# A new order for the opening of a retention-and-two-MLPs kernel: loads, first products, masks, and where the retention units are visited

## The chip, the core and the metric

The kernel runs on one core of one Trainium2 chip. The metric is the device time of one launch in microseconds (us), taken as the median of the runs shown.

## What is computed

Retention (a decaying running sum of outer products of keys and values, read by queries) over 768 steps, for 4 batches and 8 heads of 64; its output, 3072 tokens of 512 features, goes through two two-layer networks. Weights arrive as 64-bit floats.

```
state = zeros(B, H, D, D)
for t in range(S):                                  # S = 768, D = 64
    state = gamma * state + k[t] (outer) v[t]       # gamma = 1 - 2**(-5-h), per head h
    y[t] = q[t] @ state / sqrt(D)
x = y as (3072, 512)
h = x @ w_in1;  x = (h * cos(h)) @ w_out1           # 512 -> 2048 -> 512
h = x @ w_in2;  out = where(h > 0, h, exp(min(h, 0)) - 1) @ w_out2
```

## The kernel before

**Tiling.** Tokens are cut into 6 blocks of 512 and 24 units of 128 (4 units to a block). The hidden width of 2048 is cut into 8 tiles `j` of 256. Products of fp32 quality are made from three TensorE products of a high and a low part (`PARTS`), so the first layer's product for one block, one `j` and one half (128 hidden features) takes 12 matmuls of 128x512, four chunks of three. They stand on line 778 (`product1`). From about 329 us on, TensorE does the second layers and the second network (lines 862 and 1039) by a seven-product scheme.

**Units.** A unit of retention is worked off in steps that each use 64x64 tiles of TensorE: `scores` (keys against queries, line 639, and for later units the sums of keys and values, line 594), `carried` (queries against the running state, line 693) and `values` (line 728). The function `meet` is a *visit*: it does `carried` of unit n, `scores` of unit n+1 and `values` of unit n, then loads unit n+3. VectorE multiplies the scores by a mask (line 658), GpSimd writes one small fence per unit between `carried` and `values` (line 705), and ScalarE and VectorE split the result into high and low parts (lines 365 and 370). The first four units are special: for them a unit is one chunk of 128 features over all four batches, so chunk `kc` of block 0 needs unit `kc` alone. The sums of these four (`first_sums`, line 594) are taken in two pairs, each pair in a PSUM buffer of its own that VectorE then copies to the state (line 615).

**Weights.** `to_f32` loads a half of a weight tile as raw 64-bit words (512 KB), ScalarE makes two passes over it, a third pass runs on GpSimd (line 410) for three halves of the opening and on ScalarE otherwise, and VectorE joins them (line 417). `first_weights` then splits the tile into high and low parts.

**What sets the order.** A planner (`Plan.run`) takes the steps in the order in which the code records them, gives each a due time, and writes the instructions of every engine. TensorE's order is the recorded one. In the opening the load queue goes by ranks (`opening`). Zero products (`warm`, line 1116) fill TensorE's idle time at the start. Buffers come from pools: in PSUM, `eg` has three buffers (scores, sums, hidden products) and `f` has two (zeros, `carried`/`values`, second layer). The function `dma` sends nearly all loads and stores through SP's queue (line 360), and a load waits for the one eight places ahead of it.

**Where visits stand.** A list of (block, half step, function, unit) at the end of the code puts a visit in front of a half product or between its two halves. Units 6 and 23 are split: their `carried` is a visit of its own.

## Time and profile before

| what | value |
|---|---|
| median of 3 runs | 1020.47 us (1020.46 to 1022.87) |
| profiled execution | 1020.92 us, span 1019.1 us |
| TensorE busy | 1011.3 us, 99% of the span |
| VectorE busy | 780.0 us, 77% |
| ScalarE busy | 636.2 us, 62% |
| GpSimd busy | 163.1 us, 16% |
| granted TensorE clock | 1.00 |

The span runs from the first to the last instruction of the profiled execution; 1.8 us of its time lie around the span. A busy share is an average over stages, and the stage that the change touches is the first 330 us, and of that mostly the first 30. In the rows, a line of the timeline gives the start, the length of the group, the engine, the line, the operation with its output and inputs, and in brackets how long the engine sat idle before it and who ended that. One 64x64 product of the program stands as two records, so a step of 16 products shows as x32.

### The profile page before, as it was taken

What the parts mean: (1) busy time and instruction counts of PE and PEld (TensorE: products, weight loads), DVE (VectorE), ACT (ScalarE), POOL (GpSimd) and SP (SyncE); (2) the same over time, 40 slices, a digit from 0 to 9 for tenths busy, and PEclk for the clock granted to TensorE, in tenths of its full rate; (3) what the DMA queues carried; (4) which work ended last, traced back from release to release, by engine and by line L of the source; (5) the groups of instructions that cost most, each with busy time, mean ns of one, the idle gap of its engine ahead of it and who ended that gap; (6) DMA issues with size and microseconds to landing.
All of it is one profiled execution on the core that took longest, in us unless ns stands there. A gap on an engine that the chain in (4) does not pass through costs nothing.

```text
span 1019.1 us, 17949 instructions
## 1 busy us (share of the span) xinstructions
PE 1011.3 (99%) x7088; PEld 831.1 (82%) x7090; DVE 780.0 (77%) x928; ACT 636.2 (62%) x801; POOL 163.1 (16%) x163
## 2 busy tenths in 40 slices
PE   8999999999999999999999999999999999999998
PEld 5888888888888888888888888888888888888887
DVE  7998887798699768566669998978899866565453
ACT  5985458655896544444455788988998644444442
POOL 2222321222032101000001242332221100000000
PEclk9999999999999999999999999999999999999999
DMA  9997999999999999999977579899968999999862
GB/s 349 354 341 291 353 334 379 345 351 357 335 363 342 340 344 333 367 320 357 350 231 254 208 255 340 303 335 350 337 248 303 315 365 335 361 316 349 286 201 88
DMA packets 110244, 323.17 MB, mean 317 GB/s; under 512 B 8657, under 2 KB 9041, under 8 KB 107601
## 3 DMA queue, kind: packets, MB, share of 16 engines
q1 hardware_dynamic: 110016, 321.95, 88.5%
q8 instruction: 55, 0.90, 0.4%
q14 instruction: 29, 0.23, 0.1%
q10 hardware_dynamic: 144, 0.10, 0.0%
HBM read 195.66 MB, written 126.35 MB: 316 GB/s over the span
## 4 chain that ended last, share of the span: by engine, by line
PE 98%; DMA 2%; DVE 0%; POOL 0%; SPq 0%; issue 0%; POOLq 0%
PE eg L1039 45%; PE eg L778 26%; PE eg L862 16%; PE f L862 6%; DMA c<-in_weights 2%; PE f L693 1%; PE eg L594 1%; PE f L728 1%; PE eg L639 1%; POOL c L410 0%; PE eg L728 0%; SPq L360 0%; DVE c L417 0%; DVE hl L370 0%; DVE h L370 0%
## 5 line engine op out<-in xcount | busy, mean ns | idle before, releaser
L1039 PE MATMUL eg<-hl,w 128*128 128x512 f32 (+1 forms) x2022 | 457.4, 388 | 0.0
L1039 PEld LDWEIGHTS eg<-hl,w 128*128 128x128 f32 x2022 | 378.8, 188 | 78.4
L365 ACT ACTIVATE hl<-ld 128x1024 fp32r<-128x1024 f32 x168 | 177.8, 1060 | 221.0 <-PE eg L1039 218.5
L370 DVE TENSOR_TENSOR hl<-ld,hl 128x1024 fp32r<-128x1024 f32 x168 | 209.8, 1252 | 129.0 <-ACT hl L365 128.4
L778 PE MATMUL eg<-hl,w 128*128 128x512 f32 x1152 | 269.5, 392 | 0.7 <-DVE hl L370 0.7
L778 PEld LDWEIGHTS eg<-hl,w 128*128 128x128 f32 x1152 | 214.0, 188 | 46.8 <-DVE hl L370 1.0
L365 ACT ACTIVATE c<-c 128x512 f32<-128x512 f32 (+3 forms) x197 | 160.1, 850 | 29.5 <-DVE c L370 13.5
L370 POOL TENSOR_TENSOR c<-c 128x512 f32<-128x512 f32 (+2 forms) x91 | 101.2, 1118 | 434.4 <-DMA c<-d 164.3
L365 ACT ACTIVATE c<-eg 128x1024 int32<-128x1024 f32 (+2 forms) x95 | 86.5, 910 | 57.4 <-PE eg L778 49.8
L370 DVE TENSOR_TENSOR c<-c 128x512 f32<-128x512 f32 (+2 forms) x161 | 109.7, 692 | 16.2 <-DMA c<-d 9.9
L862 PE MATMUL eg<-hl,w 128*128 128x512 f32 x432 | 109.5, 390 | 0.0
L862 PEld LDWEIGHTS eg<-hl,w 128*128 128x128 f32 x432 | 80.9, 188 | 17.5 <-DVE c L370 0.4
L862 PE MATMUL eg<-ld,w 128*128 128x512 f32 x288 | 73.2, 390 | 0.0
L809 DVE SCALAR_TENSOR_TENSOR c<-eg,c 128x1024 f32<-128x1024 f32 x48 | 58.6, 1221 | 18.0 <-ACT c L365 17.7
L365 ACT ACTIVATE c<-c,quarter_turn 128x1024 f32<-128x1024 f32 x48 | 55.2, 1150 | 25.6 <-DVE c L809 24.9
L370 DVE TENSOR_TENSOR c<-c,eg 128x1024 f32<-128x1024 f32 x48 | 58.3, 1215 | 12.5 <-ACT c L365 12.2
L862 PEld LDWEIGHTS eg<-ld,w 128*128 128x128 f32 x288 | 53.9, 188 | 11.8 <-ACT h L365 0.6
L365 ACT ACTIVATE w<-c 128x1024 fp32r<-128x1024 f32 (+3 forms) x63 | 54.2, 886 | 12.9 <-DVE c L370 5.3
L485 DVE SCALAR_TENSOR_TENSOR w<-c,w 128x1024 fp32r<-128x1024 f32 (+3 forms) x51 | 54.2, 1077 | 2.0 <-ACT w L365 2.0
L365 ACT ACTIVATE ends<-c 128x512 int16<-128x512 uint32 x64 | 50.0, 787 | 2.3 <-DMA c<-in_weights 2.3
L862 PE MATMUL f<-hl,w 128*128 128x512 f32 x144 | 36.6, 389 | 0.0
L862 PE MATMUL f<-ld,w 128*128 128x512 f32 x144 | 36.5, 389 | 0.0
(76 smaller groups left out, 675.4 us busy)
## 6 DMA issues: line engine op xcount, KB each, us to landing
d<-c SPq DMA_DIRECT2D x205, 512.0 KB, 5.2
ld<-d SPq DMA_DIRECT2D x84, 1024.0 KB, 8.3
c<-d SPq DMA_DIRECT2D x93, 512.0 KB, 6.3
c<-in_weights SPq DMA_DIRECT2D x64, 512.0 KB, 6.8
ld<-in_attn SPq DMA_DIRECT2D x19, 1024.0 KB, 7.0
d<-h SPq DMA_DIRECT2D x48, 256.0 KB, 6.4
out<-c SPq DMA_DIRECT2D x11, 512.0 KB, 7.9
ld<-in_attn SPq DMA_DIRECT2D x3, 512.0 KB, 7.6
```

What stands on the lines that cost most here:

```text
L365: plan.op("ACT", us, lambda: bank_of(nc.scalar.activation(out=out_(), in_=in_(), func=func, **kw), r), r, w, lag)
L370: return bank_of(e.tensor_tensor(out=out_(), in0=a(), in1=b(), op=op), r)
L485: plan.op("DVE", 0.065 + 0.267 * (hi - lo), lambda: nc.vector.scalar_tensor_tensor(out=w.t[:, lo:hi, 1, :], in0=view(), scalar=turn, in1=h ...
L594: nc.tensor.matmul(out=sc.t[j * D:(j + 1) * D, e, lo:lo + D], lhsT=u.t[r, 1536 + h0:1536 + h0 + D], rhs=u.t[r, 1024 + h0:1024 + h0 + D], s ...
L639: ins = nc.tensor.matmul(out=sc.t[e * HC:(e + 1) * HC, j, at:at + cols], lhsT=u.t[r, 512 + h0 + cs * HC:512 + h0 + cs * HC + HC], rhs=u.t[ ...
L693: ins = nc.tensor.matmul(out=xps[e].t[o * D:(o + 1) * D, a2, ch * HC:(ch + 1) * HC], lhsT=s[r, e * 2 + a2, :], rhs=q[r, 2 * a2 + e, ch * H ...
L728: ins = nc.tensor.matmul(out=x_out(e)[o * D:(o + 1) * D, a2, lo:lo + cols], lhsT=u.t[r, h0:h0 + D], rhs=pt_of()[r, j, at:at + cols], start ...
L778: nc.tensor.matmul(out=h.t[:, half * TB:(half + 1) * TB], lhsT=quarter(j, quads[kc // 2], wpart, kc % 2), rhs=(xh, xl)[xpart].t[:, kc, :], ...
L809: plan.op("DVE", 1.134, lambda: nc.vector.scalar_tensor_tensor(out=g.t, in0=h.t, scalar=1.0 / TWO_PI, in1=n(), op0=ALU.mult, op1=ALU.subtract,
L862: bank_of(nc.tensor.matmul(out=out_(), lhsT=w.t[:, i, wpart, kc * P:(kc + 1) * P], rhs=x.t[:, xpart, kc, :], start=(start and n == 0), sto ...
L1039: bank_of(nc.tensor.matmul(out=to.t[:, at:at + c1 - c0], lhsT=w[:, A_OF[p], wpart, i * P:(i + 1) * P], rhs=hl.t[:, gpart, k, c0:c1], start ...
```

## The change

- **First loads** go by a table, `FIRST_LOADS`, in place of the order unit by unit.
- **First queries unscaled.** The first four units' queries are no longer multiplied by the decay table; the decay of the query's row goes into the masks, whose tables are built from a new small table (`rise`) with VectorE and two ScalarE copies. The decay table itself is loaded and built later.
- **First products** go by `FIRST_PRODUCTS`: the scores first, 16 zeros behind the first, and the products of `j` 0 and 1, chunk by chunk, all ahead of the first sums (before: `j` 0 alone).
- **First slices by quarters.** The quarters of the first tiles are packed in another order, and the tile of `j` 1 is split in two steps as that of `j` 0 was; GpSimd does the third pass for five halves, not three.
- **First values** use the two small `f` buffers in place of one `eg` buffer, and are split in two halves on ScalarE and VectorE.
- **Odd blocks in reverse**: blocks 1 and 3 go through `j` from 7 to 0, and the results of `j` 5 to 7 of the block before stay in SBUF (`HELD`), so that six loads of 512 KB fall away.
- **Visits** stand in a table with 24 entries in place of 25: unit 6 is no longer split.
- The planner counts the cost of a change between small and full TensorE tiles. This changes no instruction by itself.

```diff
+FIRST_LOADS = (
+    ("tab",), ("qk", 1), ("qk", 0), ("v", 0), ("w", 0, 0), ("qk", 2), ("w", 1, 0), ("k", 1),
...
+FIRST_PRODUCTS = (
+    ("s", 0), ("z", 16), ("s", 1), ("x", 0), ("s", 2), ("x", 1),
+    ("h", 0, 1, (0,)), ("z", 4), ("x", 2), ("h", 0, 0, (0,)), ("s", 3), ("h", 0, 0, (1,)),
...
+HELD = 3
+VISITS = (
+    (4, "sums_of", 0), (4, "sums_of", 2), (5, "scores_of", 4), (6, "meet", 4), (8, "meet", 5),
...
-            if (layer, io) == (0, 0) and (j, hh) in ((0, 0), (0, 1), (1, 0)):
+            if (layer, io) == (0, 0) and (j, hh) in BY_POOL:
...
-        ends = [4 * j + 2] * (j == 0) + [4 * j + 4]
+        ends = [4 * j + 2] * (j < 2) + [4 * j + 4]
...
-        xps = xps_of.pop(n) if c else [Buf("eg", [P, 2, TB])]
+        xps = xps_of.pop(n) if c else [Buf("f", [P, 2, P]) for _ in range(2)]
...
-        for e in range(2) if c else (slice(0, 2),):
+        for e in range(2):
...
-        quads = ((0, 1), (3, 2))[fi]
+        quads = ((0, 2), (1, 3))[fi]
...
+            if sb < NSB - 1 and j >= NJ - HELD:
+                held[j] = g
...
-        y = Buf("c", [P, 2 * TB])
+        y = held.pop(j, None)
         t4 = Buf("h", [P, TB])
-        dma(4, lambda: y.t, lambda: gd[layer, sb].t[:, j, 2:4, :],
-            [gd[layer, sb][j * NP + 2, j * NP + 4]], [y], lag)
+        if y is None:
+            y = Buf("c", [P, 2 * TB])
+            dma(4, lambda: y.t, lambda: gd[layer, sb].t[:, j, 2:4, :],
+                [gd[layer, sb][j * NP + 2, j * NP + 4]], [y], lag)
...
+        for at, by in ((0, by_own), (1, by_late)):
+            tt("DVE", 0.37, lambda at=at, slots_at=slots_at: slots_at(at), up, by, ALU.mult,
+               [rise, tab_at, cst[604, 740]], [own])
+        tt("DVE", 0.37, lambda slots_at=slots_at: slots_at(0), lambda slots_at=slots_at: slots_at(0),
+           lambda: tri(2, 2), ALU.mult, [own, tab_at], [own])
+        act(0.33, lambda slots_at=slots_at: slots_at(2), lambda slots_at=slots_at: slots_at(0), [own], [own])
...
-    warm(12)
-    scale_unit(0, which=(0,))
+    warm(ZEROS)
...
+    first_h = [Buf("eg", [P, 2 * TB]) for _ in range(2)]
+    for name, n, *at in FIRST_PRODUCTS:
...
-    split = (6, 23)
...
+            j = NJ - 1 - at if blk in (1, 3) else at
```

What that does to the engines is shown at three places.

SP's queue, the first loads, before. `ld_123`, `ld_144`, `ld_156` and `hl_193` are units 0 to 3, and `c_...` are weight halves; a row of 1024 is queries and keys, one of 512 is values or, the second time, the keys by token.

```order
L360 DMA ld_123<-in_attn 128x1024
L360 DMA ld_123<-in_attn 128x512
L360 DMA c_142<-in_weights 128x1024
L360 DMA ld_144<-in_attn 128x1024
L360 DMA ld_144<-in_attn 128x512
L360 DMA c_150<-in_weights 128x1024
L360 DMA ld_156<-in_attn 128x1024
L360 DMA ld_156<-in_attn 128x512
L360 DMA hl_193<-in_attn 128x1024
L360 DMA hl_193<-in_attn 128x512
```

The same place after; units 0 to 3 are `ld_123`, `ld_141`, `ld_148` and `hl_227`, and the seventh row is unit 1's keys by token.

```order
L393 DMA ld_123<-in_attn 128x1024
L393 DMA ld_141<-in_attn 128x1024
L393 DMA ld_123<-in_attn 128x512
L393 DMA c_144<-in_weights 128x1024
L393 DMA ld_148<-in_attn 128x1024
L393 DMA c_172<-in_weights 128x1024
L393 DMA ld_141<-in_attn 128x512
L393 DMA ld_148<-in_attn 128x512
L393 DMA ld_141<-in_attn 128x512
L393 DMA w_121<-in_tab 128x96
L393 DMA c_207<-in_weights 128x1024
L393 DMA hl_227<-in_attn 128x1024
```

Unit 1's values were the fifth load and are now the ninth; unit 0's queries and keys are the first in both, though the table names unit 1 first.

TensorE, the first sums, before, with what each waits for (DVE is VectorE, Pool GpSimd, DMAHW a load).

```order
L594 MATMUL eg<-ld 64x64 [waits DMAHW5_49,PE_49,Pool_49]
L594 MATMUL eg<-ld 64x64 x15
L594 MATMUL eg<-ld 64x64 [waits DMAHW6_49]
L594 MATMUL eg<-ld 64x64 x15
L594 MATMUL eg<-ld 64x64 [waits DMAHW7_49,PE_49]
L594 MATMUL eg<-ld 64x64 x15
L594 MATMUL eg<-hl 64x64 [waits DMAHW0_49]
L594 MATMUL eg<-hl 64x64 x15
```

The same place after.

```order
L626 MATMUL eg<-ld 64x64 [waits DMAHW0_49,PE_49]
L626 MATMUL eg<-ld 64x64 x15
L626 MATMUL eg<-ld 64x64 [waits DMAHW7_49,Pool_49]
L626 MATMUL eg<-ld 64x64 x15
L626 MATMUL eg<-ld 64x64 [waits DVE_49,DMAHW7_49,PE_49,Pool_49]
L626 MATMUL eg<-ld 64x64 x15
L626 MATMUL eg<-hl 64x64 [waits DMAHW1_49]
L626 MATMUL eg<-hl 64x64 x15
L808 MATMUL eg<-hl,w 128x512 [waits DVE_49]
```

The third unit's sums wait for VectorE now: two of the three `eg` buffers hold hidden products, and the second pair takes the buffer of the first, which VectorE has to copy out.

TensorE, two visits in the middle of the first network, before: the small steps of a visit and the products between.

```order
L693 MATMUL f<-ld,w 64x64 x16
L594 MATMUL eg<-ld 64x64 x16
L639 MATMUL eg<-ld 64x64 x16
L728 MATMUL f<-w,ld 64x64 x16
L778 MATMUL eg<-hl,w 128x512 x24
```

After, at the visits with the table's 36, 37 and 40.

```order
L725 MATMUL f<-ld,w 64x64 x16
L626 MATMUL eg<-ld 64x64 x16
L671 MATMUL eg<-ld 64x64 x16
L759 MATMUL f<-w,ld 64x64 x16
L808 MATMUL eg<-hl,w 128x512 x12
L725 MATMUL f<-ld,w 64x64 x16
L626 MATMUL eg<-ld 64x64 x16
L671 MATMUL eg<-ld 64x64 x16
L759 MATMUL f<-w,ld 64x64 x16
L808 MATMUL eg<-hl,w 128x512 x36
```

Some visits stand 12 products apart now; before, none behind the opening stood closer than 24.

## Rows read from the trace of the kernel before

**Rows 1.** The page, part 1: busy us, share of the span, instructions.

```profile
PE 1011.3 (99%) x7088; PEld 831.1 (82%) x7090; DVE 780.0 (77%) x928; ACT 636.2 (62%) x801; POOL 163.1 (16%) x163
```

**Rows 2.** TensorE by stretches: us, busy (instructions), granted clock, DMA share, GB/s.

```profile
10.00:20.00 10.00, 9.24 (x208) 1.00 1.04 404
20.00:30.00 10.00, 9.29 (x187) 1.00 1.02 399
30.00:300.00 270.00, 270.00 (x3489) 1.00 0.95 344
```

**Rows 3.** All that TensorE waited for: us in total, times, longest.

```profile
PE eg L639 <- DVE ld L370: 2.0, 2, 1.8
PE f L1116 <- DVE c L1119: 1.2, 1, 1.2
PE eg L778 <- DVE hl L370: 0.7, 1, 0.7
PE eg L639 <- PE eg L728: 0.5, 1, 0.5
```

**Rows 4.** Timeline of TensorE in the opening.

```profile
7.64 0.90 PE L639 MATMUL eg<-ld 64*64 64x128 f32 x32 [1.79 <-DVE ld L370]
8.47 1.90 PE L1116 MATMUL f<-c 128*128 128x512 bf16 x7
...
25.91 1.63 PE L594 MATMUL eg<-ld 64*64 64x64 f32 x96
27.36 0.65 PE L594 MATMUL eg<-hl 64*64 64x64 f32 x32
```

**Rows 5.** Timeline of SP's queue, stretches 0.7 to 1.0, 5.5 to 5.9, 5.95 to 6.4.

```profile
0.73 0.39 SPq L360 DMA_DIRECT2D ld<-in_attn  x1
...
5.62 0.33 SPq L360 DMA_DIRECT2D ld<-in_attn  x1
...
5.99 0.43 SPq L360 DMA_DIRECT2D hl<-in_attn  x1
```

**Rows 6.** Loads issued in those stretches: count, KB, us from issue to landing.

```profile
ld<-in_attn SPq DMA_DIRECT2D x1, 512.0 KB, 4.7
...
ld<-in_attn SPq DMA_DIRECT2D x1, 256.0 KB, 7.9
...
hl<-in_attn SPq DMA_DIRECT2D x1, 512.0 KB, 8.8
```

**Rows 7.** Timeline of VectorE: masks, conversions, first copies of sums.

```profile
11.52 0.96 DVE L658 TENSOR_TENSOR w<-eg,c 128x768 f32<-128x768 f32 x1
12.39 0.68 DVE L370 TENSOR_TENSOR w<-c,w 128x512 fp32r<-128x512 f32 x1
12.99 0.69 DVE L370 TENSOR_TENSOR ld<-ld,w 128x512 f32<-128x512 f32 x1
...
27.14 0.76 DVE L615 COPY w<-eg 128x256 f32<-128x256 f32 x2 [0.34 <-PE eg L594]
27.82 1.22 DVE L809 SCALAR_TENSOR_TENSOR c<-eg,c 128x1024 f32<-128x1024 f32 x1
...
42.79 1.51 DVE L417 SCALAR_TENSOR_TENSOR c<-c,ends 128x512 uint32<-128x512 uint32 x1
```

**Rows 8.** Timeline of GpSimd and ScalarE: third pass, a scaling, first passes.

```profile
11.74 1.54 POOL L410 TENSOR_SCALAR c<-c 128x512 f32<-128x512 f32 x1 [1.45 <-DMA c<-in_weights]
...
41.45 2.30 POOL L370 TENSOR_TENSOR ld<-ld,w 128x512 f32<-128x512 f32 x2 [0.16 <-DVE w L370]
...
7.89 1.42 ACT L365 ACTIVATE c<-c 128x512 int16<-128x512 uint32 x2 [5.22 <-DMA c<-in_weights]
```

**Rows 9.** The chain that ended last, 76 to 106 us: start, us, what.

```profile
78.77 0.47 PE f L728 x32
79.24 11.11 PE eg L778 x48
90.35 0.62 PE f L693 x32
```

**Rows 10.** Groups of GpSimd: busy us, mean ns of one, idle before them.

```profile
L370 POOL TENSOR_TENSOR c<-c 128x512 f32<-128x512 f32 (+2 forms) x91 | 101.2, 1118 | 434.4 <-DMA c<-d 164.3 <-DVE c L965 77.0 <-ACT w L365 47.1
...
L705 POOL MEMSET fences<- 1x1 f32 x20 | 1.8, 89 | 118.8 <-PE f L693 118.8
```

## The prediction

> **What bounds the kernel now.** I read the page first, then the stretches, the waits and the chain, and last the timeline of the opening. TensorE is busy for 99% of the span [rows 1]. By stretches it is full from 30 us on, at a granted clock of 1.00 [rows 2], and everything that it ever waited for is over by 21 us: 4.4 us in four groups, of which 3.2 us lie behind its start [rows 3]. So after the opening the time is the number of products, and the change leaves that as it is: as many full-tile products and as many small ones in both programs. What can move is (a) the opening up to the first sums, (b) how often TensorE changes between full and small tiles, and (c) new waits where there are none.

> In the opening, waits are not the only loss. TensorE also runs 16 zeros behind the first scores, the first 8 of them in 1.90 us [rows 4], so some 3.6 us; with the 3.2 us of waits, 6.8 us is all that any order of the opening could win.

> **The change, part by part.**

> *Loads.* The queue of loads is the pace of the opening: its engines are busy throughout between 10 and 30 us [rows 2]. The first 512 KB land at 0.73 + 4.7 = 5.4 us; unit 2's values, behind 3422 KB, at 5.62 + 7.9 = 13.5; the next 512 KB at 5.99 + 8.8 = 14.8 [rows 5, 6]. So 512 KB take 1.3 us there. Before, unit 1's values were the fifth load; now eight loads stand ahead of them (three of 512 KB of queries and keys, two weight halves, unit 0's values, unit 1's keys by token and unit 2's values), with the table and themselves 3698 KB. That lands at 13.5 + 276/512 x 1.3 = 14.2 us by the pace of the rows; at an even 1.3 us per 512 KB from the first landing on it would be 13.3. I take 14.2, since the same queue set both rows. The keys by token are not needed before the first sums and cost these values 0.65 us.

> *First scores and masks.* Unit 0's scores start at 5.9 us, when the 12 zeros end, and not at 7.64 behind the scaling of the queries [rows 4]: 1.8 us earlier. That is won only if what follows is early too. Each score or value step takes 0.83 us with the change of tiles behind it (7.64 to 8.47) [rows 4]. Scores 0, 16 zeros, scores 1, values 0 and scores 2 end at about 12.7 us. The masks now need more small VectorE steps ahead of the first one; they end near 10 us, before values 0 ask. The mask of unit 1 stands behind the join of the first weight half: landing near 9.7, two ScalarE passes in 1.42 us beside 1.54 us on GpSimd [rows 8], the join 0.69, the mask 0.96 [rows 7], so 13.0 us. Values 1 thus wait for their load, from 12.7 to 14.2: this wait takes the place of the one of 1.79 us.

> *From there to the first sums.* Three value steps and one score step, 4 x 0.83 = 3.3 us; 48 products of 0.227 us, 10.9; four entries into full tiles at 0.23, 0.9 (48 products took 11.11 us with one entry [rows 9]); 4 zeros, 0.9. These zeros now draw on the same two small buffers as the values, so they wait until VectorE has split unit 1: about 0.4 us. Sum 16.4, first sums at 30.6 us. Before, they start at 25.9 with 24 products done; the other 24 take 5.4, so the same point is 31.3. **Gain 0.7 us.**

> *The first sums.* Before, the four sums run through without a gap, 25.91 to 28.0 [rows 4]. Now the second pair waits until VectorE has copied the first pair out: 0.76 us for the two copies [rows 7] and 0.3 for handing over both ways. **Loss 1.1 us**, more if a step of 1.22 us is just under way on VectorE [rows 7]. The products of `j` 2 behind it wait for the low part of their weights: 0.2.

> *One run of small steps fewer.* A run of small steps costs 0.23 us on the way out and 0.62 - 0.47 = 0.15 on the way in [rows 9]. **Gain 0.4 us.** Behind the opening there are 24 runs before and 23 after; the steps themselves are all still there.

> *At nothing.* The six loads that fall away, the smaller first-value steps and the reversed order: the queue is waited on by nobody behind the opening [rows 3], and the held results occupy three of ten buffers that then take no load. If that cover were gone, a weight half would come 1.3 us late.

> *GpSimd beside VectorE.* VectorE's join took 1.51 us in place of 0.69 beside a GpSimd product of two SBUF operands [rows 7, 8]. The reordered opening puts two such scalings of GpSimd between 13 and 22 us, beside VectorE's splits. Not at all or both in full would be 0 to 1.6 us; I take 0.3, because VectorE works with some slack there.

> Sum: -0.7 + 1.1 + 0.2 - 0.4 + 0.3 = +0.5 us. The profiled execution took 1020.92, so it would become 1021.4; the median lies 0.45 below it, so **1021.0 us, no change that can be told**.

> **The rivals.**

> *Faster.* The values land at 13.3 and values 1 start with the mask (0.9 less), the zeros don't wait (0.4), a free VectorE and a late second pair hide the sums' gap (1.1), nothing is lost beside GpSimd (0.5). That is 1021.0 - 2.9 = 1018.1 us. For it: the even pace holds in parts of the queue. Against: the second pair's wait is in the program, and two copies take what they take. Chance 0.12, a third of it beyond 0.3%.

> *Conversions block VectorE.* If each third pass on GpSimd held VectorE's two-operand steps as its products do, the two added passes would cost up to 0.8 us each on the path from the weights to the masks: 1021.0 + 1.6 = 1022.6. The rows speak against: beside the pass from 11.74 to 13.28 us [rows 8] VectorE's steps at 12.39 and 12.99 took 0.68 and 0.69, not lengthened [rows 7]. [...] Chance 0.08.

> *Slower: visits too close.* Seven gaps between runs of small steps are 12 products long now, 2.7 us; before, none behind the opening was shorter than 24, 5.4 us. In such a gap VectorE has to form the mask, the new state and the splits, and GpSimd the fence. Before, GpSimd waited for TensorE at all 20 fences, 118.8 us in all [rows 10], so they had room. A GpSimd product of 1.12 us in front of the fence [rows 10], or a step of 1.22 on VectorE, makes TensorE wait about 1.1 us. One or two such waits leave the forecast standing; from three on the loss passes 0.3%, and five of seven give 1021.0 + 5.5 = 1026.5. Against: the planner keeps GpSimd free ahead of a fence, and several visits stood 24 products apart with no wait at all [rows 3]. Chance 0.10.

> *The order does nothing.* Unit 0 comes first anyway, zeros fill what is won, and the loads set the pace: then only the sums' gap and the saved run are left, +0.7 us, 1021.2. This lies within the forecast's range.

> **How the numbers follow.** Forecast (with the last rival) 0.70, faster 0.12, conversions 0.08, too close 0.10. The bounds of the forecast alone are the load (0.9 less), the zeros (0.4 less) and VectorE beside GpSimd (0.3 less to 1.3 more), so 1019.4 to 1022.3; to hold 8 in 10 the range takes in the conversions and most of the faster case: 1018.4 to 1022.8. About 0.3%, 3.06 us, is what a measurement of this kernel can tell from no change. Faster than that: a third of the faster case and a little for what I have not seen, 0.07. Slower: the close visits and a little more, 0.11. Same: 0.82.

> **What the profile after would show.** Scores 0 at 5.9 us; an idle time of 1 to 2 us ahead of unit 1's values, ended by a load; a short one ahead of the second group of zeros, ended by VectorE; first sums at 30 to 31 us with a gap of about 1.1 us ahead of the third unit's, ended by VectorE's copies; and no wait of TensorE between 40 and 330 us. First sums before 29 us or no gap in them would make me wrong on the fast side; idle time of TensorE ahead of `carried` or `values` at the close visits (near 33, 143, 162, 191 and 250 us) on the slow side.

## The result, and the profile after

The changed kernel takes 1035.36 us (1034.34 to 1035.79), the kernel before 1021.34 (four runs, 1020.46 to 1022.87): 1.0134 times as long, interval 1.0117 to 1.0152. It is slower by 14.0 us, and the time lies outside my range. The profiled execution took 1035.54 us with a span of 1033.8, 14.7 more than before.

The page, part 1 (busy us, share of the span, instructions) and one row of part 3 (queue: packets, MB, share of 16 engines), of after:

```profile
PE 1016.1 (98%) x7092; PEld 834.9 (81%) x7094; DVE 770.2 (75%) x912; ACT 636.7 (62%) x806; POOL 187.8 (18%) x183
q8 instruction: 55, 0.90, 0.3%
```

TensorE has as many instructions as before [rows 1], and its share has fallen from 99% to 98%. The last row plays no part in my prediction. It is what this case is about: 55 packets of 16 KB, which I take to be TensorE's: it has 14,186 weight loads and matmuls, 258 to a packet. The page of before has the same 55 packets and 0.90 MB, so it is not their number that changed.

By stretches (us, then busy and count of TensorE, its weight loads, VectorE, ScalarE, GpSimd, then granted clock, DMA share, GB/s):

```profile
30.00:300.00 270.00, 258.79 (x3538) 212.65 (x3537) 212.56 (x298) 175.63 (x248) 68.20 (x78) 0.99 0.88 315
...
170.00:175.00 5.00, 3.18 (x10) 2.43 (x10) 0.81 (x2) 1.46 (x3) 1.28 (x1) 0.81 0.98 351
...
210.00:215.00 5.00, 5.00 (x16) 3.94 (x15) 1.27 (x2) 1.02 (x1) 0.73 (x1) 0.66 0.99 365
```

Between 30 and 300 us, where TensorE was full before [rows 2], it is idle for 11.2 us, and in two places the granted clock is below 1.00. All that TensorE waited for (us in total, times, longest):

```profile
PE f L759 <- issue: 4.1, 2, 3.3
PE eg L808 <- issue: 3.3, 1, 3.3
PE eg L626 <- issue: 1.4, 1, 1.4
PE eg L671 <- issue: 1.3, 1, 1.3
PE f L759 <- DMA ld<-in_attn: 1.3, 1, 1.3
...
PE eg L626 <- DVE w L647: 1.1, 1, 1.1
PE f L1153 <- DVE hl L403: 0.7, 1, 0.7
```

The last three are the waits of the opening that I had announced. The first four are new against [rows 3], 10.1 us in five stops, and "issue" says that nothing which the profile shows was waited for: no semaphore, no load, no other engine. I call such an idle time a stop. The chain of waits around two of them (start, us, what):

```profile
163.53 2.95 PE eg L808 x12
166.47 0.62 PE f L725 x32
167.10 0.53 PE eg L626 x32
167.63 0.47 PE eg L671 x32
168.10 0.47 PE f L759 x31
168.57 3.25 issue
171.82 0.21 PE f L759
172.03 26.32 PE eg L808 x108
...
205.35 1.12 PE eg L808 x4
206.48 3.29 issue
209.77 15.39 PE eg L808 x60
```

The first stop is ahead of the last of a visit's 128 small matmuls, the second 4 products behind the end of a visit. In the listings of the order a wait stands at the first instruction of a step, and these stops are in the middle. The products behind run late as well: 108 took 26.32 us, where 108 at 0.227 and one change of tiles at 0.23 make 24.7 (in the trace of before 24 products with their change of tiles take 5.67 us, from 50.14 to 55.81, and 48 take 11.11 [rows 9]), and the first 60 behind the second stop took 15.39, where 60 at 0.227 make 13.6. That is 3.4 us lost at a lower clock: 0.50 was granted from 173.1 to 176.5 us and from 210.7 to 214.0, and 1.00 ahead of both and behind them.

So the 14.7 us are 10.1 of stops, 3.4 of clock behind the two longest, and 1.0 of the opening: the visit with 72 products done starts at 41.39 us, and at 40.42 before. That leaves 0.2.

### The profile page after: what moved, and what is told of

The parts are those of the page before. It is cut to its first block, busy times and chain, and to the rows that moved or that the text cites. A ratio compares the mean times of both kernels' runs of the same rounds, so it can differ in the third digit from the quotient of the medians.

```text
span 1033.8 us, 17983 instructions
## 1 busy us (share of the span) xinstructions
PE 1016.1 (98%) x7092; PEld 834.9 (81%) x7094; DVE 770.2 (75%) x912; ACT 636.7 (62%) x806; POOL 187.8 (18%) x183
## 4 chain that ended last, share of the span: by engine, by line
PE 97%; issue 1%; DMA 1%; DVE 0%; SPq 0%; POOL 0%; ACT 0%; POOLq 0%
PE eg L1076 44%; PE eg L808 26%; PE eg L899 16%; PE f L899 6%; PE f L725 1%; PE f L759 1%; PE eg L626 1%; PE eg L671 1%; DMA c<-in_weights 1%; SPq L393 0%; POOL c L442 0%; DVE c L449 0%; PE f L1153 0%; DVE w L647 0%; DVE c L403 0%
## 5 line engine op out<-in xcount | busy, mean ns | idle before, releaser
L403 POOL TENSOR_TENSOR c<-c 128x256 f32<-128x256 f32 (+1 forms) x109 | 125.9, 1161 | 445.3 <-DMA c<-d 151.2
L398 ACT ACTIVATE c<-c 128x512 f32<-128x512 f32 (+4 forms) x197 | 158.8, 842 | 27.9 <-DVE c L403 18.0
L403 DVE TENSOR_TENSOR c<-c 128x512 f32<-128x512 f32 (+2 forms) x143 | 96.4, 682 | 23.0 <-DMA c<-d 15.7
L840 DVE SCALAR_TENSOR_TENSOR c<-eg,c 128x1024 f32<-128x1024 f32 x48 | 58.6, 1221 | 27.1 <-ACT c L398 25.6
L403 POOL TENSOR_TENSOR h<-c 128x512 f32<-128x512 f32 x15 | 20.4, 1362 | 145.9 <-DMA d<-h 129.9
L398 ACT ACTIVATE h<-eg 128x512 f32<-128x512 f32 x50 | 29.5, 590 | 11.8 <-PE eg L1076 7.9
## 6 DMA issues: line engine op xcount, KB each, us to landing
ld<-d SPq DMA_DIRECT2D x84, 1024.0 KB, 8.5
ld<-in_attn SPq DMA_DIRECT2D x19, 1024.0 KB, 6.9
```

Of the source, the lines that this page charges most:

```text
L398: plan.op("ACT", us, lambda: bank_of(nc.scalar.activation(out=out_(), in_=in_(), func=func, **kw), r), r, w, lag)
L403: return bank_of(e.tensor_tensor(out=out_(), in0=a(), in1=b(), op=op), r)
L840: plan.op("DVE", 1.134, lambda: nc.vector.scalar_tensor_tensor(out=g.t, in0=h.t, scalar=1.0 / TWO_PI, in1=n(), op0=ALU.mult, op1=ALU.subtract,
```

## Experiments

**Count of instructions.** Counting TensorE's records in the trace of after (weight loads, matmuls, semaphore instructions), 768, 3328, 768 and 1024 stand between one stop and the next: 3, 13, 3 and 4 times 256. In the window from 169.2 to 169.3 us, 0.7 us into the stop that begins at 168.57, the trace has one packet of the instruction queue:

```profile
q8 instruction: 1, 0.02, 68.6%
```

Work goes on at 171.82, 2.6 us behind its start. The packets at the other four stops start at 41.4, 59.1, 207.3 and 266.4 us, and work goes on 2.4 us behind each.

### The visits' places alone, both ways

In the changed kernel the old places from the table's 10 on, with unit 6 split again:

```diff
-    (10, "meet", 6), (12, "meet", 7), (19, "meet", 8), (21, "meet", 9), (24, "meet", 10),
...
+    (10, "carried", 6), (12, "meet", 6), (14, "meet", 7),
+    (16, "meet", 8), (20, "meet", 9), (24, "meet", 10), (28, "meet", 11),
...
```

> The changed kernel with all its other parts, but from the table's 10 on the visits stand where they stood before (unit 6 split again, no gap under 24 products). Theory 'instructions run out': TensorE gets its instructions in blocks of 256 (16 KB each, by DMA), and two visits 12 products apart use up blocks faster than they arrive; with gaps of 24 the idle of 10 us with no releaser falls to 0 to 2 us, the granted clock is 1.00 throughout, and the time is 1020.5 to 1023. Rival 'close visits wait for VectorE or GpSimd': also about 1021. Rival 'another part' (opening, reversed blocks, held results): the loss stays, 1033 to 1036.

Measured: 1023.53 us, 1.0025 of before (1.0015 to 1.0035), just above my 1020.5 to 1023. So 11.8 us of the loss are the places' and 2.6 remain. Of its waits one is left with no releaser:

```profile
PE f L761 <- DVE hl L405: 1.5, 1, 1.5
...
PE eg L628 <- DVE w L649: 1.1, 1, 1.1
...
PE eg L628 <- issue: 0.9, 1, 0.9
```

It stands at 43 us, within two instructions of the count at which the first stop of after stands, in the part of the table that this kernel shares with it. "Another part" is out as the main loss.

Then the new places in the kernel before:

```diff
-        (1, 12, meet, 11), (2, 2, meet, 12), (2, 4, meet, 13), (2, 8, meet, 14), (2, 13, meet, 15), (3, 0, meet, 16),
...
+        (2, 4, meet, 13),
+        (2, 5, meet, 14),
+        (2, 8, meet, 15),
+        (2, 9, meet, 16),
...
```

> The kernel before with nothing changed but the visits' places, which are those of the changed kernel. Theory 'instructions run out': stops of 0.5 to 3.3 us with no releaser in or just behind the second visit of close pairs, 6 to 14 us in all, clock below 1.00 behind the long ones, 1028 to 1036. Rival 'close visits wait for VectorE or GpSimd': as long, but at every close pair alike and with VectorE or GpSimd as releaser. Rival 'another part': no stops, 1020 to 1022.

Measured: 1033.48 us, 1.0124 (1.0107 to 1.0141). The size is the theory's, the cause is not. The waits of TensorE, and behind them the two longest at close visits:

```profile
PE f L693 <- DVE hl L370: 5.2, 5, 2.3
PE eg L639 <- DVE ld L370: 2.2, 1, 2.2
PE eg L594 <- DVE ld L370: 1.6, 1, 1.6
...
PE f L728 <- POOL fences L705: 1.1, 2, 0.6
PE eg L778 <- issue: 0.7, 1, 0.7
...
154.27 0.90 PE L594 MATMUL eg<-ld 64*64 64x64 f32 x32 [1.62 <-DVE ld L370]
173.05 0.95 PE L693 MATMUL f<-ld,w 64*64 64x64 f32 x30 [2.26 <-DVE hl L370]
```

Here close visits do wait for VectorE's splits, as the recorded rival has it: 5.9 us at the second visits of three of the five close pairs (the other two have no wait). The waits for GpSimd's fence, 1.1 us, and 0.9 us more for VectorE stand at visits with 24 products or more ahead of them; the second row is the opening's. Only 0.7 us are stops, at the block border at which the changed kernel stops for 3.3 us, and behind the wait of 2.26 us. Run alone, this experiment would have settled the matter wrongly. I take it that where VectorE spaces the visits out, the instructions have time to come.

### The same visits, other block borders

The places stay, and the borders of the blocks are moved against them by zeros that are narrower and more, the same work in more instructions. In the changed kernel the 16 zeros behind the first scores:

```diff
-            for _ in range(n):
-                nc.tensor.matmul(out=rest_ps.t, lhsT=rest.t[:, 0:P], rhs=rest.t, start=True, stop=True)
+            cols = TB // 4 if n == 16 else TB
+            for _ in range(n * TB // cols):
+                nc.tensor.matmul(
+                    out=rest_ps.t[:, 0:cols], lhsT=rest.t[:, 0:P], rhs=rest.t[:, 0:cols], start=True, stop=True)
```

> The changed kernel with every visit in its place; the 16 zero products behind the first scores become 64 of a quarter of the width, the same work in 96 instructions more (a product is a weight load and a matmul). Theory 'instructions run out': the stops sit at fixed numbers of the instruction stream, so they move to other work: none at 58 to 62, at 206 to 210 and at 267 to 269 us, a new one near 151 to 155, 3 to 9 us of idle in all, 1025 to 1033. Rivals 'wait for VectorE or GpSimd' and 'another part': the stops stay at the same five places, 10 us, 1034 to 1036.

Measured: 1027.34 us (1026.41 to 1030.17), 8.0 less than the changed kernel; 1030.17 is the profiled execution. Its stops behind the opening:

```profile
47.64 5.37 PE L808 MATMUL eg<-hl,w 128*128 128x512 f32 x23 [2.28 <-issue]
171.12 0.47 PE L671 MATMUL eg<-ld 64*64 64x64 f32 x17 [2.21 <-issue]
205.06 0.39 PE L671 MATMUL eg<-ld 64*64 64x64 f32 x11 [0.28 <-issue]
```

They are at other work than before. Those at 58 to 62 and 267 to 269 us are gone, that at 206 to 210 is down to 0.28, and 10.1 us have become 4.8. The place that I had named, 151 to 155 us, was wrong: I can tell where a border falls, not how late its block is.

In the kernel before, all 28 zeros of the opening (the same edit with `TB // 4 if n > 4 else TB // 2`):

> The kernel before with every visit in its place; the 28 zero products of the opening become 96 narrower ones (a quarter of the width, the two groups of 4 a half), the same work in 136 instructions more. Theory 'instructions run out': with the block borders moved against the visits, stops with no releaser appear in a kernel that had none, 1 to 7 us in all, most likely near 79 and 145 us: 1022 to 1029. Rivals 'wait for VectorE or GpSimd' and 'another part': no stop behind 31 us, 1020.5 to 1022.

Measured: 1029.75 us, 1.0074 (1.0047 to 1.0101), with no visit moved; that is above my 1022 to 1029. The profiled execution is the shortest of its four, 1024.32 us, and shows two stops, within 3 us of the places named:

```profile
81.06 0.44 PE L728 MATMUL f<-w,ld 64*64 64x64 f32 x11 [1.53 <-issue]
147.89 0.27 PE L728 MATMUL f<-w,ld 64*64 64x64 f32 x1 [0.71 <-issue]
```

Both rivals had no stop here. The kernel before was close to the limit too, and its borders fell well. The other executions, 1029.6 to 1030.7, I take to have longer stops at the same borders. Their mean granted clocks of 0.996 to 0.998, against 1.000 in the profiled one, fit that, but no profile of them exists, so it is not shown.

A shift that should have been better than none:

```diff
-    warm(12)
+    warm(16)
...
-                nc.tensor.matmul(out=rest_ps.t, lhsT=rest.t[:, 0:P], rhs=rest.t, start=True, stop=True)
+                nc.tensor.matmul(out=rest_ps.t[:, 0:P], lhsT=rest.t[:, 0:P], rhs=rest.t[:, 0:P], start=True, stop=True)
```

> The kernel before with every visit in its place, and 200 instructions more in the opening (all zeros a quarter of the width, four times as many, and 16 in place of the first 12), so that no block of 256 has to follow the one before within less than 7.4 us, where the kernel before has three blocks at 5.3 to 5.8. Theory 'instructions run out': no stop, runs closer together than the 1020.1 to 1022.9 of before, 1020.0 to 1021.0. If more instructions in the opening were themselves the loss of the last shifted kernel: 1025 to 1031 again.

Measured: 1022.83 us (1022.06 to 1024.75), 1.0020 (1.0012 to 1.0029): neither better than before nor closer together, so my 1020.0 to 1021.0 was missed, and 1025 to 1031 did not come either. Behind 31 us there is no stop, as expected, but in the opening there is one:

```profile
21.28 0.34 PE L728 MATMUL eg<-w,ld 64*64 64x64 f32 x7 [1.41 <-issue]
```

The 128 narrow zeros are themselves 256 instructions, in groups of 6.46, 1.96, 1.07 and 1.07 us, and the inputs load meanwhile (DMA share 1.04 between 10 and 20 us). I had looked at the borders behind the opening only.

### Less traffic

TensorE's instructions stay the same one by one, three quarters of the stores are left out:

```diff
-        dma(2 * (hi - lo), lambda: gd[layer, sb].t[:, j, lo:hi, :], src, r,
+        part = slice(0, P if layer else 32)
+        dma(2 * (hi - lo), lambda: gd[layer, sb].t[part, j, lo:hi, :], lambda: src()[part], r,
...
-        dma(4, lambda: k.t, lambda: t.t, [t], [k], lag)
+        dma(4, lambda: k.t[0:32], lambda: t.t[0:32], [t], [k], lag)
```

> The changed kernel, TensorE's instructions the same one by one; left out is three quarters of each store of the first network's results and of the converted weights (32 of 128 partitions are written, what reads them later reads as many bytes of an input), so the queue carries about a third less between 30 and 300 us. Theory 'instructions run out, because their blocks wait behind the data': the idle with no releaser falls from 10 us to 0 to 3, the granted clock stays at 1.00, 1020.5 to 1025. Rival 'blocks come at a pace of their own' (the traffic has no part in it): 8 to 11 us of idle stay, 1033 to 1036.

Measured: 1027.14 us (1024.04 to 1028.84), 8.2 less than the changed kernel; the profiled execution took 1027.46, with a span of 1024.0.

```profile
168.22 0.21 PE L759 MATMUL f<-w,ld 64*64 64x64 f32 x1 [2.07 <-issue]
203.21 31.90 PE L809 MATMUL eg<-hl,w 128*128 128x512 f32 x140 [1.91 <-issue]
...
30.00:300.00 270.00, 264.75 (x3582) 218.17 (x3581) 221.29 (x307) 183.47 (x259) 71.17 (x82) 1.00 0.69 219
```

With a DMA share of 0.69 in place of 0.88, two of the five stops are gone, a third is down to 0.18 us, the two longest have shrunk from 3.3 to 2.0, and the clock stays at 1.00 in this execution. The three that are left stand at the counts of instructions of three stops of the changed kernel, within two. The time lies between my two expectations, and so do the 4.2 us of stops: the traffic makes the blocks late, and a part of the price is left with less of it.

### The price of a block

384 extra 64x64 products that nothing reads, twice (in the rows each is two matmuls):

```diff
+    def probe(n):
+        ps = [Buf("f", [P, TB]) for _ in range(2)]
...
+            for m in range(n):
+                r, c = m % 2 * HC, m // 2 % 2 * HC
+                nc.tensor.matmul(
+                    out=ps[m % 2].t[c:c + HC, 0:HC], lhsT=zero.t[r:r + HC], rhs=zero.t[r:r + HC], start=True, stop=True,
```

> The kernel before with two runs of 384 extra 64x64 zero products that nothing reads, in the form of a visit's products: 1536 instructions each, six blocks of 256. One run stands between two visits near 128 us, with the queue full, one behind the last product, with the queue nearly empty. At a visit's pace (128 matmuls in 2.3 us) each run would take 14 us. Theory 'instructions run out': TensorE stops at every block border; a block costs 5 to 8 us near 128 us and about 4.5 us at the end, so 30 to 48 us and about 27 us, and the launch takes 1075 to 1100 us. Rival 'the supply is not the limit': no stops, 28 us for both, 1049 us.

Measured, in two runs: 1064.11 us, 43.4 more than before and less than my 1075 to 1100. The first run, with the queue full at its start, and the second, behind the last product:

```profile
126.52 2.09 PE L1130 MATMUL f<-zero 64*64 64x64 f32 x127
129.82 2.09 PE L1130 MATMUL f<-zero 64*64 64x64 f32 x128 [1.21 <-issue]
136.56 3.56 PE L1130 MATMUL f<-zero 64*64 64x64 f32 x128 [4.65 <-issue]
142.76 3.32 PE L1130 MATMUL f<-zero 64*64 64x64 f32 x128 [2.64 <-issue]
146.76 2.09 PE L1130 MATMUL f<-zero 64*64 64x64 f32 x128 [0.68 <-issue]
150.21 2.09 PE L1130 MATMUL f<-zero 64*64 64x64 f32 x128 [1.36 <-issue]
...
1055.08 2.09 PE L1130 MATMUL f<-zero 64*64 64x64 f32 x128 [1.38 <-issue]
```

In the first run there is a stop behind every 128 matmuls, 256 instructions with their weight loads, and nowhere else. From block to block it takes 3.3, 6.7, 6.2, 4.0, 3.5 and 3.7 us near 130 us, and 3.5 to 4.0 at the end. The long ones are those with a full queue; the rest of the kernel waits for this run, and the queue runs dry:

```profile
137.00:144.00 7.00, 4.36 (x184) 4.22 (x180) 0.00 (x0) 0.00 (x0) 0.00 (x0) 0.74 0.97 346
144.00:154.00 10.00, 6.32 (x336) 5.81 (x328) 0.00 (x0) 0.00 (x0) 0.00 (x0) 0.87 0.06 22
```

So a block cost 3.5 to 4 us almost without traffic (DMA share 0.06) and up to 6.7 with it (0.99 between 126 and 137 us). My 4.5 and 5 to 8 were too high, and the two runs took 27.4 and 18.4 us rather than 30 to 48 and 27. (The second began with 264 matmuls that ran through; I take it that two blocks were in store or on their way.)

By this the places can be judged. A visit takes 2.0 us in the chain above (0.62, 0.47, 0.47 and 0.47) and 12 products 2.95: 280 instructions in 5.0 us, a block in 4.5. With 24 products it is 304 in 7.7, a block in 6.5. Plain products use a block in 29 us (128 at 0.227). Visits 12 apart ask for more than came with a full queue, a block in 6.2 to 6.7 us; visits 24 apart are at that limit, and the stop of after at 61 us is at one of these. But a fast block is no stop by itself. Before, the visit at 195.35 us uses up most of a block in 2 us and nothing stops; the last packet ahead of it had started at 192.6 us, in time. At the stop of 168.57 us the packet started 2.8 us behind the begin of the visit.

### The rest of the change

Without the reversed blocks and the held results:

```diff
-HELD = 3
+HELD = 0
...
-            j = NJ - 1 - at if blk in (1, 3) else at
+            j = at
```

> The changed kernel without its reversed blocks and without held results, visits in their new places. If the reversed order is the loss: 1021 to 1024. If it is what lets VectorE be in time at close visits (it was late there, 2.3 us at the most, when the places alone were changed): waits for VectorE come back at the close visits and in the first block, 3 to 9 us, with some of the stops with no releaser left, 1033 to 1044.

Measured: 1042.97 us, 7.6 more than the changed kernel.

```profile
PE eg L808 <- DVE c L403: 5.6, 1, 5.6
PE f L725 <- DVE hl L403: 5.2, 5, 3.1
PE eg L626 <- POOL w L403: 2.8, 1, 2.8
```

The five waits of the second row are at the second visits of close pairs; of stops, 1.0 us is left. The reversed order with the held results is no loss. It lets VectorE be in time at the close visits, and thereby brings the instructions to the fore. It also changes the first block, where the waits of 5.6 and 2.8 us are, so the 7.6 us are not the visits' alone.

In the kernel with the old places, the products of `j` 0 alone ahead of the first sums:

```diff
-    first_h = [Buf("eg", [P, 2 * TB]) for _ in range(2)]
+    first_h = [Buf("eg", [P, 2 * TB]) for _ in range(1)]
...
-    (4, "sums_of", 0), (4, "sums_of", 2), (5, "scores_of", 4), (6, "meet", 4),
+    (2, "sums_of", 0), (2, "sums_of", 2), (5, "scores_of", 4), (6, "meet", 4),
```

> The changed kernel with the visits where they stood before, and with the products of j 0 alone ahead of the first sums (placed at the table's 2), as before. The recorded step 'first sums' says that the second pair's wait of 1.1 us comes from the hidden products of j 1, which hold the third buffer: the wait goes, the first sums start near 25.6 us, and against the run with the old places, 1023.5, the time falls by 1 to 2 us: 1021 to 1022.5. If the wait is VectorE's copy alone, it stays and so does 1023.5.

Measured: 1021.34 us, 1.0004 (0.9995 to 1.0013), no difference from before and 2.2 less than with two tiles. But the wait went only from ahead of the second pair to behind it:

```profile
29.17 8.43 PE L808 MATMUL eg<-hl,w 128*128 128x512 f32 x36 [1.17 <-DVE w L647]
```

The products of `j` 1 now want the first pair's buffer while VectorE still copies it out. What was won lies elsewhere: the stop of 0.9 us at 43 us is gone (the scores now stand 36 products behind the sums, in place of 12, which I take to be the reason), and so are small waits of 0.39 and 0.33; the wait for unit 1's values is 0.82 us in place of 1.5.

The two pairs of sums 12 products apart:

```diff
-    (2, "sums_of", 0), (2, "sums_of", 2), (5, "scores_of", 4), (6, "meet", 4),
+    (2, "sums_of", 0), (3, "sums_of", 2), (4, "scores_of", 4), (6, "meet", 4),
```

> The changed kernel with the visits where they stood before, j 0 alone ahead of the first sums, and the two pairs of sums 12 products apart (the table's 2 and 3), so that VectorE copies the first pair out under products. Recorded step 'first sums': both the gap ahead of the second pair and the one behind the pair go, 1.2 us less than with the pairs side by side (1021.34) and 0.4 more for one run of small steps: 1020.3 to 1020.9. If a wait only moves again: 1021.2 to 1022.

Measured: 1021.57 us, 1.0010 (1.0001 to 1.0019). The gap at the sums is gone, there is no wait of that kind left, and the time has not fallen. In the profiled execution (1022.31 us) the wait for unit 1's values is 1.74 us, and the granted clock is 0.83 between 10 and 20 us, which eats what the sums gave. The other ten executions had a granted clock of 1.000 and are no faster than with the pairs side by side, so the clock is not the reason there; it stays open. No kernel here beats the one before.

## Why the prediction was wrong

**What bounds the kernel.** "After the opening the time is the number of products" is the step that failed, and with it "no wait of TensorE between 40 and 330 us": the runs showed 10.1 us of stops there and 3.4 us lost to a granted clock of 0.50 behind them. Full and free of waits are not the same as unlimited: behind TensorE's 100% stood a supply of instructions that it used nearly up, and I counted products and small steps, never instructions per microsecond. A row that could have told is in part 3 of the page of before, 0.90 MB of instructions; with 256 to a block, a visit 12 products behind another asks for a block in 4.5 us, on DMA engines that were 95% busy [rows 2].

**The rival "visits too close"** had the sign and the kind of place, and a wrong cause for this kernel. Its mechanism is real for VectorE: with the new places alone it is late by 5.9 us in all at close visits, where I had 5.5. GpSimd's fence was late at none of them. In the changed kernel it is not the one that ends last. At 0.10 the chance was too small: I set seven new gaps of 12 products against "the planner keeps GpSimd free" and against waits that were absent at gaps of 24, which says nothing of 12.

**Loads, first scores, zeros.** Confirmed, within 0.4 us each: unit 1's values start at 14.12 us, ended by a load (14.2 forecast); the scores at 6.16 (5.9); the zeros wait 0.71 for VectorE (0.4). The sums start at 31.03 rather than 30.6. So the gain there is 0.3 us and not 0.7. The 0.2 us for the weights of `j` 2 did not show.

```profile
14.12 0.90 PE L759 MATMUL f<-w,ld 64*64 64x128 f32 x32 [1.33 <-DMA ld<-in_attn]
...
31.03 1.16 PE L626 MATMUL eg<-ld 64*64 64x64 f32 x64
33.27 0.69 PE L626 MATMUL eg<-ld 64*64 64x64 f32 x32 [1.08 <-DVE w L647]
```

**First sums.** Confirmed: 1.08 us, ended by VectorE's copies (1.1). The cause was the shared buffers, as said, but taking the second hidden tile away only moves the wait.

**The other rivals.** "Faster" needed a late second pair and values 1 before 14 us; neither came. (It also took off 0.5 us beside GpSimd, where the sum has 0.3.) "The order does nothing" was nearer for the opening, 1.0 us late at the same visit, than my sum.

**One run fewer, `j` 2's weights, GpSimd beside VectorE, conversions.** None was tested alone. Values 1 waited for their load, not for a mask held up by conversions.

**At nothing: the reversed blocks.** Wrong in this company: without them and the held results the changed kernel takes 7.6 us more. I asked who waits for the queue, and not what VectorE no longer has to wait for.

With the old places the sum of +0.5 us stands against +2.6 (1.5 to 3.6): besides the gain that was 0.4 smaller, the stop of 0.9 us and two small waits of 0.7 together are what it lacked.

## What to carry to other kernels

Count instructions, not only work: where TensorE runs many small tiles in a row, compare the time in which it uses up 256 instructions with the 3.5 to 6.7 us that a block cost here. An idle time in the middle of a step, with no releaser, is a sign of it; counting instructions between two such stops (here multiples of 256) ties it to the blocks, and shifting the stream by harmless instructions tests it. A fast block is a warning and no verdict: with a packet that had started 2.8 us ahead of the visit nothing stopped here, with one that started 2.8 us behind its begin TensorE stopped for 3.3 us. A kernel may be free of such stops only because its block borders fall well, so an unrelated edit ahead can cost much of what a bad one does (8.8 us here, against 14.0), and a change of places is best judged with the supply of instructions counted in.

## What the runs showed of the hardware

- The trace of after has 55 packets of 16 KB (0.90 MB) on the instruction queue q8 while the kernel runs, which I take to be TensorE's (14,186 weight loads and matmuls, 258 to a packet). Between its stops stand 768, 3328, 768 and 1024 of TensorE's instructions, and in the first of the added runs a stop followed every 256. With a DMA share of 0.69 in place of 0.88 the stops fell from 10.1 to 4.2 us. A block cost 3.5 to 4 us at a DMA share of 0.06, up to 6.7 at 0.99.
- Work went on 2.3 to 2.6 us behind the start of the late packet, at each of the five stops of after.
- Behind the stops of 3.3 us the granted clock fell (0.81 and 0.66 over 5 us): it was 0.50 for 3.4 us behind each. Behind 4.65 us in the added run it was 0.74 over 7 us. Of the two stops of 2.2 to 2.3 us in the shifted kernel one was followed by a fall (0.77 over 5 us), the other was not, nor were those of 2.07 and 1.91 us with less traffic. So the two stops of 3.3 us cost half as much again as they lasted: 3.4 us of clock for 6.5 of the two.
